# Counting SyncE's issue time per load as measured in a build-time ordering

## The chip, the cores and the metric

The kernel runs on one core of one Trainium2 chip. The metric is the time of one execution on the device in microseconds (us). A trace shows one execution, taken by the hardware profiler; its span is some 2 us shorter than the time of that execution. In it PE is TensorE's matmuls, PEld TensorE's weight loads, DVE VectorE, ACT ScalarE, POOL GpSimd, and SP SyncE. SyncE only issues transfers. A "landing" is the moment at which a transfer's data has arrived and its semaphore is raised.

## The reference

Threshold attention over 8 batches of 8 heads, 576 positions and 64 dimensions, then a gated feed-forward block with a folded RMS norm on the 4608 tokens:

```python
scores = scale * np.matmul(q, k.transpose(0, 1, 3, 2))
thresh = np.max(scores, axis=-1, keepdims=True) - tau           # tau = 0.02
scores = np.where(scores >= thresh, scores, -1e9)
attn = softmax(scores)
x = np.matmul(attn, v)                     # then heads to the last axis: [4608, 512]
xn = x / rms(x) * rms_g
g, val = xn @ w_gate, xn @ w_val           # 512 -> 1536
return (g * sigmoid(g) * val) @ w_out      # 1536 -> 512
```

## The kernel before

The scores are computed in fp32, the rest of the matmuls in fp16. Every piece of work is an `Op` with an engine, a cost in ns, a priority and its dependencies. A list scheduler puts them all into one order at build time. It walks through a model of the engines and always takes the op that can start first. Only that order goes to the chip. Each engine then runs its instructions in that order and waits on semaphores for what the model misjudged.

```python
COST = dict(
    s_main=932.0, s_virt=900.0, tr_qk=530.0, tr4=230.0, ...
    sp=350.0, sp_tr=1300.0, sp_qk=1310.0, sp_tl=630.0,
)
DMA_NS = dict(qk=1250.0, tl=700.0, v=880.0, vt=350.0, wt=1700.0, ..., w=820.0, wo=2500.0)
...
def order_ops(ops, ring_sizes):
    ...
                if o.bulk:                                   # loads: at most 3.5 us of transfers outstanding
                    t = max(t, dma_free - BACKLOG)
                k = (t + (BIAS if other else 0.0), o.prio, i)
    ...
        eng_free[e] = t + cost
        if o.dma:
            dma_free = max(dma_free, t + 300.0) + o.dma      # one pipe for all transfers
            o.end = max(dma_free, t + o.cost) + (LAT_TR if o.cost == COST["sp_tr"] else LAT_LD if o.bulk else 2000.0)
```

q and k are loaded in natural layout, k first and q after it. TensorE transposes them in groups of 16 (8 for k, then 8 for q) with priority -500, that is, as soon as the model takes both loads to have landed. v and the feed-forward weights are loaded on the same SyncE queue.

```python
def emit_qk(b, p, prio):                       # pair p of heads, batch b
    for j, src in ((1, k), (0, q)):
        def load(o, j=j, src=src):
            for h in range(2):
                nc.sync.dma_start(out=nat[:, j, :, h], in_=src[b, 2 * p + h, 0:MAIN].rearrange(...))
        los.append(gated(add("SP", COST["sp_qk"], prio - 3, before, load, dma=DMA_NS["qk"], bulk=True), prio - 3))
    def tr(o):                                 # 16 small fp32 transposes into two PSUM banks
        for j in (1, 0):
            for c in range(4):
                for r, rs in enumerate(HALF):
                    nc.tensor.transpose(ring[o.slot[r]][:, at:at + 64], nat[rs, j, c].rearrange(...), id32[rs, rs])
    t = gated(add("PE", COST["tr_qk"], -500.0, los + [o_id] + ..., tr, ring="R", nring=2, mode=1), prio)
...
def emit_v(b, prio):
    lo = gated(add("SP", COST["sp"], pr, ..., load, dma=DMA_NS['v'], bulk=True), pr)
...
# 24 weight loads
lo = gated(add("SP", COST["sp"], pr, w_use[slot][-1:], load, dma=DMA_NS['w'], bulk=True), pr)
...
seq = order_ops(ops, {"R": 4})
with tc.manual_schedule():
    for o in seq:
        o.fn(o)
```

A *step* below is one of 144 softmax steps. It begins with a *burst* of eight score matmuls (`s_ps<-qkt`). Transposes of the attention weights (`ring<-id,wsb`), attention-times-value matmuls (`ring<-va,wt`) and feed-forward groups (`ring<-xnT,wg`) fill the space between bursts.

## Time and profile before

| what | value |
|---|---|
| time, median of 3 runs (range) | 572.69 us (572.63 to 573.38) |
| span of the profiled run (its time) | 569.2 us (571.37 us) |
| busy PE / ACT / DVE | 98% / 81% / 75% |
| first and last score matmul of a main burst | 6.4 and 505.9 us |

The profile is shown in the prediction, line by line. In a time line a row is the start in us, the length in us, engine, source line, operation, output and inputs, and how many instructions. The square bracket is the idle time of the engine just before, with the releaser that the profile infers.

### The profile page before, as it was taken

The page shows a single profiled execution, that of the slowest core. Times are in us where ns is not written, and L with a number is a line of the kernel's source. Part 1 is how long each engine was busy: PE and PEld are TensorE (multiplying, and loading weights), DVE is VectorE, ACT ScalarE, POOL GpSimd, SP SyncE. Part 2 cuts the span into 40 slices and gives each one's busy share as a digit, 9 for nine tenths or more (in the row PEclk, how much of TensorE's full clock was granted, in tenths as well). Part 3 has the DMA queues.
Part 4 walks back from the last instruction along what each step waited for, and adds up shares of the span by engine and source line. Part 5 has one row for each costly group of instructions (what it writes and reads, how often), then busy time and mean ns, then how long its engine had stood idle before and what let it go on. Part 6 is the DMA issues. An engine that isn't in the chain of part 4 may idle for free.

```text
span 569.2 us, 13800 instructions
## 1 busy us (share of the span) xinstructions
PE 558.1 (98%) x5000; PEld 335.6 (59%) x5000; DVE 427.7 (75%) x1093; ACT 458.9 (81%) x739; POOL 322.2 (57%) x462
## 2 busy tenths in 40 slices
PE   8989999999999999999999999999999999999996
PEld 4666776767667555555555455555555555554674
DVE  4898986969868588858984888668974887486354
ACT  4998889998879888989888899789897898783331
POOL 2368956875657456665666557666674665451000
PEclk9999999999999999999999999999999999999999
DMA  7999999778896678889996688879977645641211
GB/s 180 233 271 261 227 172 218 142 121 186 184 200 121 130 149 158 186 181 162 175 180 157 134 168 174 186 176 176 179 157 185 95 94 106 141 107 30 75 39 37
DMA packets 271172, 89.00 MB, mean 156 GB/s; under 512 B 253696, under 2 KB 263424, under 8 KB 271104
## 3 DMA queue, kind: packets, MB, share of 16 engines
q1 hardware_dynamic: 268304, 86.02, 72.6%
q0 software_dynamic: 1600, 1.57, 1.9%
q8 instruction: 39, 0.64, 0.5%
q10 hardware_dynamic: 1200, 0.52, 0.3%
q14 instruction: 29, 0.24, 0.2%
HBM read 37.75 MB, written 9.44 MB: 83 GB/s over the span
## 4 chain that ended last, share of the span: by engine, by line
PE 88%; DVE 4%; DMA 3%; ACT 1%; SPq 1%; issue 1%; POOL 1%; ACTq 0%; DVEq 0%
PE s_ps L568 27%; PE ring L794 15%; PE ring L799 15%; PE ring L855 15%; PE ring L699 6%; PE ring L304 2%; DMA qkn<-in_q_dram 2%; PE ring L695 2%; DVE ssb L591 2%; PE s_ps L794 1%; PE s_ps L833 1%; PE s_ps L855 1%; PE ring L661 1%; PE s_ps L799 1%; ACT ssb L609 1%
## 5 line engine op out<-in xcount | busy, mean ns | idle before, releaser
L591 DVE CUSTOM_DVE_ANT_0 ssb<-s_ps,zrow 128x576 f32<-128x576 f32 x288 | 207.1, 753 | 56.6 <-PE s_ps L568 45.4
L609 ACT ACTIVATE ssb<-ssb,nth 128x576 f32<-128x576 f32 x224 | 165.4, 765 | 25.3 <-POOL nth L598 24.9
L568 PE MATMUL s_ps<-qkt 64*128 64x288 f32 x1024 | 170.9, 430 | 1.4 <-DVE mx L591 1.2
L568 PEld LDWEIGHTS s_ps<-qkt 64*128 64x128 f32 x1024 | 95.9, 186 | 53.0 <-DVE mx L591 16.8
L642 POOL TENSOR_SCALAR wsb<-ssb,nth 128x576 f16<-128x576 f32 x64 | 110.5, 1726 | 11.2 <-ACT esb L628 3.5
L799 PE MATMUL ring<-xnT,wv 128*128 128x512 f16 (+1 forms) x544 | 111.8, 328 | 0.1
L794 PE MATMUL ring<-xnT,wg 128*128 128x256 f16 (+1 forms) x540 | 111.0, 328 | 0.2 <-DVE hf L816 0.2
L598 POOL TENSOR_SCALAR nth<-mx 128x2 f32<-128x2 f32 x144 | 31.6, 220 | 126.9 <-DVE mx L591 116.7
L811 DVE SCALAR_TENSOR_TENSOR sl<-th,ring 128x512 f32<-128x512 f32 (+1 forms) x135 | 74.5, 552 | 28.8 <-ACT th L808 28.3
L616 ACT ACTIVATE wsb<-ssb 128x1152 f16<-128x1152 f32 x80 | 92.9, 1162 | 2.0
L808 ACT ACTIVATE th<-ring 128x512 f32<-128x512 f32 (+1 forms) x135 | 65.3, 485 | 31.0 <-PE ring L794 27.3
L855 PE MATMUL ring<-wo,hf 128*128 128x512 f16 x384 | 89.3, 380 | 0.0
L647 POOL TENSOR_TENSOR wsb<-wsb,esb 128x576 f16<-128x576 f16 x64 | 81.8, 1278 | 10.7 <-ACT esb L628 6.5
L816 DVE TENSOR_TENSOR hf<-ring,sl 128x512 f16<-128x512 f32 (+1 forms) x136 | 76.1, 560 | 12.0 <-PE ring L799 2.3
L794 PEld LDWEIGHTS <-wg 128*128 128x128 f16 x576 | 51.4, 98 | 45.0 <-issue 16.2
L799 PEld LDWEIGHTS <-wv 128*128 128x128 f16 x576 | 52.8, 98 | 39.7 <-issue 8.1
L855 PEld LDWEIGHTS <-hf 128*128 128x128 f16 x408 | 37.6, 98 | 47.1 <-issue 6.2
L699 PE MATMUL ring<-va,wt 128*128 128x65 f16 (+1 forms) x1264 | 52.8, 193 | 0.0
L628 ACT ACTIVATE esb<-ssb,nth 128x576 f16<-128x576 f32 x64 | 49.1, 767 | 3.3 <-POOL nth L598 3.2
L699 PEld LDWEIGHTS <-wt 128*128 128x128 f16 (+1 forms) x1280 | 48.7, 100 | 3.8
L613 ACT ACTIVATE wsb<-ssb 128x576 f16<-128x576 f32 x64 | 43.6, 681 | 1.5
L695 PE MATMUL ring<-va,wt 128*128 128x130 f16 (+1 forms) x158 | 35.1, 227 | 0.0
(68 smaller groups left out, 451.4 us busy)
## 6 DMA issues: line engine op xcount, KB each, us to landing
vst<-in_v_dram SPq DMA_DIRECT2D x32, 256.0 KB, 3.4
qkn<-in_k_dram SPq DMA_DIRECT2D x62, 128.0 KB, 3.2
out_dram<-osb SPq DMA_DIRECT2D x31, 256.0 KB, 2.6
qkn<-in_q_dram SPq DMA_DIRECT2D x56, 128.0 KB, 3.2
stage<-in_moe_w_gate_dram SPq DMA_DIRECT2D x12, 256.0 KB, 4.1
stage<-in_moe_w_val_dram SPq DMA_DIRECT2D x12, 256.0 KB, 4.4
wt<-wsb SPq DMA_TRANSPOSE x128, 3.1
wo<-in_moe_w_out_dram POOLq DMA_DIRECT2D x4, 384.0 KB, 6.1
```

The source lines that it names most:

```text
L568: nc.tensor.matmul(s_ps[h][rows, ROW_AT + n * part:ROW_AT + n * part + n], lhs(hs), kT[i][p][h][hs, n * part:n * part + n], start=True, st ...
L591: nc.vector.tensor_tensor_reduce(out=ssb[a][:, h], in0=s_ps[h][:, ROW_AT:ROW_AT + S], in1=zrow, scale=-1.0 / 8.0, scalar=3.0e38, op0=ALU.a ...
L609: nc.scalar.activation(out=ssb[a][:, h], in_=ssb[a][:, h], func=PRELU, scale=-1.0, bias=nth[m][:, h:h + 1], **PRELU_KW)
L616: nc.scalar.activation(out=wsb[s % NW], in_=ssb[a], func=AF.Exp)
L642: nc.gpsimd.tensor_scalar(out=wsb[s % NW][:, h], in0=ssb[a][:, h], scalar1=nth[m][:, h:h + 1], scalar2=None, op0=ALU.is_le)
L647: nc.gpsimd.tensor_tensor(out=wsb[s % NW][:, h], in0=wsb[s % NW][:, h], in1=esb[es], op=ALU.mult)
L699: nc.tensor.matmul(ring[o.slot[0]][rs, at:at + D + 1], w[:, 5 * h + j, rs], va[vi][:, p, 2 * j + h], start=False, stop=(h == 1 and j == 3))
L794: nc.tensor.matmul(ring[o.slot[0]][:, 0:n], wg[d][:, fs], xnT[slot][:, d, 0:n], start=(d == 0), stop=(d == 3))
L799: nc.tensor.matmul(ring[o.slot[0]][:, 0:n], wv[d][:, fs], xnT[slot][:, d, 0:n], start=(d == 0), stop=(d == 3))
L811: nc.vector.scalar_tensor_tensor(out=sl[i][:, 0:n], in0=th[i][:, 0:n], scalar=1.0, in1=ring[g.slot[0]][:, 0:n], op0=ALU.add, op1=ALU.mult)
L816: nc.vector.tensor_tensor(out=hf[hi][:, 0:n], in0=ring[vv.slot[0]][:, 0:n], in1=sl[i][:, 0:n], op=ALU.mult)
L855: nc.tensor.matmul(ring[(first or o).slot[0]], hf[hs[fc][0]][:, 128 * j:128 * (j + 1)], wo[:, fc], start=(fc == 0), stop=(fc == NFC - 1))
```

## The change

SyncE's issue time was counted as 350 ns for every plain load and store. The trace has more: 412 to 434 ns at the median for a weight load and 582 for a v load. The change counts 480, and 650 for v. The intent is that the model then expects loads later, so that transposes of q and k stand behind later score bursts and don't make TensorE wait for data. No instruction is added or removed.

```diff
-    sp=350.0, sp_tr=1300.0, sp_qk=1310.0, sp_tl=630.0,
+    sp=480.0, sp_v=650.0, sp_tr=1300.0, sp_qk=1310.0, sp_tl=630.0,
...
-            lo = gated(add("SP", COST["sp"], pr, v_cast[...] ..., load,
+            lo = gated(add("SP", COST["sp_v"], pr, v_cast[...] ..., load,
                            dma=DMA_NS['v'], bulk=True), pr)
```

More of the change, by code (lines that the diff above doesn't have):

```diff
@@ L500, in load @@
                 nc.sync.dma_start(out=nat, in_=main[:, 2 * p:2 * p + 2])
-            lo = gated(add("SP", COST["sp"], pr, v_cast[n - len(vst):n - len(vst) + 1] if n >= len(vst) else [], load,
+            lo = gated(add("SP", COST["sp_v"], pr, v_cast[n - len(vst):n - len(vst) + 1] if n >= len(vst) else [], load,
                            dma=DMA_NS['v'], bulk=True), pr)
```

## The prediction

> **What bounds the kernel now.** I read the page first: busy shares, then the 40 slices.
>
> ```profile
> span 569.2 us, 13800 instructions
> PE 558.1 (98%) x5000; PEld 335.6 (59%) x5000; DVE 427.7 (75%) x1093; ACT 458.9 (81%) x739; POOL 322.2 (57%) x462
> ...
> PE   8989999999999999999999999999999999999996
> ...
> PEclk9999999999999999999999999999999999999999
> ```
>
> TensorE has work in 558.1 of 569.2 us at full clock. All its idle time together is 569.2 - 558.1 = 11.1 us, 1.9% of the span. A change that only moves instructions about can hardly take more than that. The view of busy time by stretches tells where the idle time lies:
>
> ```profile
> 0.00:45.00 45.00, 39.89 (x378) 27.14 (x378) 34.09 (x98) 35.61 (x54) 19.63 (x45) 1.00 0.92 230
> 45.00:80.00 35.00, 34.69 (x336) 25.03 (x334) 30.70 (x88) 31.88 (x53) 27.18 (x43) 1.00 1.16 228
> 80.00:508.00 428.00, 426.67 (x3907) 247.93 (x3905) 329.97 (x837) 369.98 (x589) 272.13 (x370) 1.00 0.79 158
> 508.00:569.20 61.20, 56.84 (x389) 35.51 (x387) 32.98 (x73) 21.42 (x45) 3.28 (x6) 0.98 0.17 49
> ```
>
> (The columns are length, then busy PE, weight load, DVE, ACT, POOL, granted clock, DMA share, GB/s.) The first 45 us hold 45.00 - 39.89 = 5.1 us of idle time, and the last 61 us hold 61.20 - 56.84 = 4.4. The 463 us between hold only 11.1 - 5.1 - 4.4 = 1.6 us. The last stretch is the feed-forward drain, without loads of q, k or v, so the change has no handle on it. Next, what the transposes of q and k wait for, from the view of the tile that they read:
>
> ```profile
> L304 PE MATMUL ring<-id,qkn x448: 216/222/273, 22.5 to 423.0; 64*128 64x64 f32 x150
> ...
> its engine sat idle before it (us, times) until:
>   DMA qkn<-in_q_dram: 5.2, 5
> ```
>
> The 5.2 us count both the matmul row and the weight-load row for the same stalls (5 entries). The waits split them: 2.6 us over 3 waits on the matmul row, 2.5 over 2 on the weight-load row. So it is three places, and the time line of PE shows them:
>
> ```profile
> 22.50 0.41 PE L304 MATMUL ring<-id,qkn 64*128 64x64 f32 x8
> 23.20 0.46 PE L304 MATMUL ring<-id,qkn 64*128 64x64 f32 x8 [0.30 <-DMA qkn<-in_q_dram]
> 24.44 0.43 PE L440 MATMUL ring<-id,ktl 64*128 64x64 f32 x4 [0.77 <-DVE qkt L317]
> ...
> 36.94 0.46 PE L304 MATMUL ring<-id,qkn 64*128 64x64 f32 x8 [1.28 <-DMA qkn<-in_q_dram]
> ...
> 153.63 0.46 PE L304 MATMUL ring<-id,qkn 64*128 64x64 f32 x8 [1.05 <-DMA qkn<-in_q_dram]
> ```
>
> Each time, the k half of a transpose group has run, and the q half waits for its load. That is the prize: 0.30 + 1.28 + 1.05 = 2.6 us, plus 0.77 us for a tail transpose that waits for the DVE copy of the late group. 3.4 us in all, 0.6%.
>
> **Why the transposes stand too early.** The kernel orders its instructions at build time with a model of each engine; the change alters two constants of it. The trace has what they stand for:
>
> ```profile
> L500 SPq DMA_DIRECT2D vst<-in_v_dram x32: 415/582/2029, 7.4 to 430.2; - x32
> ...
> L918 SPq DMA_DIRECT2D stage<-in_moe_w_gate_dram x12: 327/412/628, 21.0 to 55.1; - x12
> L918 SPq DMA_DIRECT2D stage<-in_moe_w_val_dram x12: 328/434/1275, 21.7 to 61.7; - x12
> ```
>
> The model counts 350 ns for each. The medians are 582 ns (v) and 412 to 434 ns (weights), and consecutive weight loads start at 21.69, 22.17, 22.64 us, 470 to 480 ns apart. So 480 for loads and 650 for v are nearer to the chip than 350, and the model at present thinks SyncE ahead of where it is.
>
> **What the Trainium skill says.** Three places.
> - "Perfetto Trace Analysis", section "Per-instruction lifecycle: what the profiler-reported window actually captures": for a DMA issued by SP the reported window is the descriptor generation and not the data movement. The trace agrees: a q load's issues take 628 ns at the median, while the landing comes 3.2 us after issue.
> - "DMA: Bandwidth & Descriptors", section "Rules for kernel authors": issue the DMA early, compute, and wait on its semaphore late. A transpose placed later is the last third of that rule. The trace agrees in that only three of 28 such groups stall.
> - "TensorE: Matmul & The Clock Gate", section "Part 2: What happens when you issue a matmul": matmuls stay in program order and only weight loads are pulled ahead. The three stalls show it: a q half that waits stops the score bursts after it, although these read other buffers.
>
> **The change, part by part.** No instruction is added or removed, and every duration on the chip stays: 448 + 28 + 28 + 32 small fp32 transposes, 1280 score matmuls, 24 weight loads, 32 v loads, 39 stores on SyncE. Only the order on each queue can differ.
> - Model time added: 24 weight loads x 130 ns = 3.1 us, 32 v loads x 300 ns = 9.6 us, some 31 stores x 130 ns = 4.0 us; 16.7 us over the kernel.
> - Start-up: 16 weight loads and 3 v loads are issued between 16.6 and 45 us, and 4 v loads before. If SyncE is the model's bottleneck there, the later transposes shift by up to 16 x 0.13 + 7 x 0.30 = 4.2 us. But the model also charges the DMA pipe 820 ns per weight load and 880 per v load, more than the new issue times, and holds bulk loads when 3.5 us of transfers are outstanding; where that holds, the shift is nil. I take half, 2 us.
> - A softmax step in this part is some 3 us (the score bursts start at 18.04, 21.43, 25.41, 27.79 and 31.13 us), so a shift of 2 us puts most transpose groups of batch 1 behind one further score burst of 1.2 us. The 0.30 and the 1.28 us then vanish behind work that PE has anyway, and probably the 0.77. Expected: 2.35 us x 0.7 = 1.6 us.
> - Steady state: per pair of transposed inputs the added time is one v load or two, 0.3 to 0.6 us. The stall at 153.63 is 1.05 us long. A choice at a burst boundary may flip or not; I take half of it, 0.5 us.
> - A cost in turn: later transposes mean later copies to SBUF (685 ns on DVE, 567 on ACT). Batch 1 is first needed at step 16, near 57 us, and its transposes run between 22.5 and 45 us, so 3 us more lateness hits nothing. The three staging buffers free later by the same shift, which can delay a later load by a step; SyncE has waits of tens of us in front of its transposes, so I count nothing.
> - Reshuffling: the order also decides how score bursts, feed-forward groups and evacuations mesh for 500 us. PE there is full, and any new order can open or close some tenths of a us in many places. I take the mean as zero and the size as about 3 us either way, since the present tuned order leaves only 1.6 us in 463.
> Sum: -1.6 - 0.5 = -2.1 us, so 572.7 - 2.1 = 570.6 us.
>
> **The rivals.**
> 1. *Stall removed, all paid back.* In the first 80 us PE is not alone: DVE has 34.1 of 45 us and then 30.7 of 35, ACT 35.6 and 31.9. PE's weight loads wait 6.4 us for DVE's row reductions there. If the softmax chain paces that part, PE arrives earlier only to wait for DVE. For it: those waits. Against it: the lost PE time is never made up later, because PE is full from 57 us on, so work done earlier shortens the end. Time: 572 to 573.
> 2. *The order hardly changes*, because the model's DMA pipe and not SyncE sets the load times. For it: 820 and 880 ns against 480 and 650. Against it: q and k loads cost 1310 ns on SyncE against 1250 on the pipe, so SyncE counts there, and the change is described by moved transposes. Time: 572.5.
> 3. *A new wait*: a load or store that is chosen differently on SyncE stands in front of an attention-weight transpose (1306 ns each, 128 of them), and attention-times-value matmuls then wait. For it: one in-order queue, which carries everything. Against it: nearly all waits on that queue are for ACT and POOL, so it has slack. Time: 574 to 580.
> 4. *All stalls vanish*, the model now fits the chip and the drain starts earlier: 572.7 - 3.4 = 569.3, with lucky meshing 566.
>
> **Range and chances.** The middle is 570.6. The floor is near 558.1 + 4.4 + some 1.5 us before the first input lands, about 564 in the span, or 567 with the 3.5 us between span and time (572.69 - 569.2); I set the low end a little below, at 566.5. The high end, rival 3 in a mild form, is 575.0. Faster by over 2% means under 561.2, which would need PE idle time of zero: 0.01. Slower by over 2% means above 584.1, an ordering accident of 12 us: 0.03. Within 2%: 0.96.
>
> **What would show it.** Right: the waits of the q/k transposes for the q load fall from 2.6 us to under 1 on the matmul row; the score burst that stood behind the group at 36.9 now precedes it; PE idle in the first 45 us falls from 5.1 to 3 or 4; counts and mean durations of all groups are the same; PE busy stays within 2 us of 558. Wrong: waits of the same size at other transposes or on the v and weight casts, a gap on PE before the attention-times-value matmuls, or a longer drain after the last score burst (now 505.9 to 569.2 us). The prediction falls if the idle time between 80 and 508 us grows above 4 us, or if the end moves by more than the sum of the stalls.

## The result and the profile after

| | median us | range | runs |
|---|---|---|---|
| before | 573.24 | 572.63 to 575.65 | 6 |
| after | 573.86 | 573.39 to 575.79 | 6 |

The ratio of after to before is 1.0011, with a 95% interval of 0.9989 to 1.0033: the same, and if anything 0.6 us slower, where 2.1 us of gain were forecast. Ratios here are the mean time of one kernel's fast runs over the mean of the other's fast runs of the same rounds, so they are not quite the ratios of the quoted medians. Where I turn a ratio into us, I multiply its difference from 1 by the median of before.

The page of after and its busy time by stretches:

```profile
span 571.9 us, 13796 instructions
...
PE 557.3 (97%) x5000; PEld 333.3 (58%) x5000; DVE 427.6 (75%) x1093; ACT 460.2 (80%) x739; POOL 323.5 (57%) x462
```

```profile
0.00:45.00 45.00, 39.38 (x360) 26.06 (x361) 33.34 (x97) 34.13 (x53) 17.98 (x42) 1.00 0.86 216
45.00:80.00 35.00, 33.06 (x340) 24.28 (x337) 29.85 (x84) 30.57 (x50) 27.83 (x45) 1.00 1.06 219
80.00:508.00 428.00, 425.03 (x3890) 245.78 (x3887) 328.20 (x832) 368.72 (x587) 270.10 (x366) 1.00 0.79 159
508.00:571.90 63.90, 59.85 (x422) 37.20 (x420) 36.19 (x84) 26.74 (x53) 7.59 (x12) 1.00 0.20 56
```

The work is the same (PE 557.3 us against 558.1, the same number of instructions on the five engines). The columns are those of the prediction. The idle time of PE per stretch is its length minus PE's busy time (the number after the comma):

| stretch | before | after |
|---|---|---|
| 0 to 45 | 5.11 | 5.62 |
| 45 to 80 | 0.31 | 1.94 |
| 80 to 508 | 1.33 | 2.97 |
| 508 to end | 4.36 | 4.05 |
| sum | 11.11 | 14.58 |

So idle time did not shrink in the first 45 us, and new idle time came in the 463 us after that. The time line of PE in after, with its longer waits at transposes and feed-forward groups:

```profile
24.89 0.24 PE L440 MATMUL ring<-id,ktl 64*128 64x64 f32 x1 [1.43 <-DVE wt L670]
...
38.00 0.46 PE L304 MATMUL ring<-id,qkn 64*128 64x64 f32 x8 [1.26 <-DVE wt L670]
38.85 0.46 PE L304 MATMUL ring<-id,qkn 64*128 64x64 f32 x8 [0.39 <-DMA qkn<-in_q_dram]
...
53.50 0.60 PE L794 MATMUL ring<-xnT,wg 128*128 128x256 f16 x4 [1.30 <-POOL nth L598]
...
157.71 0.47 PE L304 MATMUL ring<-id,qkn 64*128 64x64 f32 x8 [0.99 <-DMA qkn<-in_q_dram]
```

One more wait, between 80 and 508 us, stands in front of an attention-times-value group:

```profile
180.75 0.22 PE L695 MATMUL ring<-va,wt 128*128 128x130 f16 x1 [1.01 <-ACT qTv L474]
```

It comes back in every other trace with the order of after (0.78 us in after_again, 1.17 in after_fix, 0.90 in after_pad_pe, all near 179 us). The order of before has none there (its second trace has one of 0.73 us at 165.83).

The releasers in the brackets have to be checked. For each of the five waits of the first list I looked for a landing of the tile that the instruction reads. There is one each time, some 0.13 us before the start: the tail of k of the batch (`ktl`) at 24.76, k of pair 2 at 37.86, q of it at 38.72, `xnT`, a transposing transfer issued at 46.90, at 53.37, and the q load at 157.58. So where the profile names DVE or POOL, it was a transfer. The same check on before changes one reading of the prediction: its 0.77 us at 24.44 "for a tail transpose that waits for the DVE copy" was a wait for the load of `ktl` too, which landed at 24.30. That load in before, read from the view of the tile:

```profile
L428 SPq DMA_DIRECT2D ktl<-in_k_dram x1: 631/631/631, 20.3 to 20.3; - x1
...
DMA to landing us min/median/max: 4.0/4.0/4.0
```

Waits of q and k transposes that a landing ended come to 0.30 + 0.77 + 1.28 + 1.05 = 3.4 us in before. In after they are 1.43 + 1.26 + 0.39 + 0.28 (at 47.23) + 0.99 = 4.35 us, and a feed-forward group that the new order starts earlier waits 1.30 us for `xnT`. The view of the tile of q and k in after says it in short, without the `ktl` stall; its idle times count matmul and weight-load rows together, as in the prediction:

```profile
L304 PE MATMUL ring<-id,qkn x448: 216/222/273, 26.0 to 431.3; 64*128 64x64 f32 x150
...
its engine sat idle before it (us, times) until:
...
  DVE wt L670: 2.7, 2
  DMA qkn<-in_q_dram: 2.2, 4
```

The group that had stalled at 22.50 to 23.20 now runs behind the next burst (at 25.98, behind the burst that starts at 24.91), and does not wait. That part worked as intended. But the tail transposes now stand alone before that burst and wait. The stall of pair 2 did not go away in this trace, although the model had been told to expect loads later. One reason is in the trace: its loads were issued later as well, and landed later still. First before, then after (the two issues of k of pair 2, for two heads):

```profile
L294 SPq DMA_DIRECT2D qkn<-in_k_dram x2: 630/686/742, 29.6 to 30.4; - x2
...
DMA to landing us min/median/max: 4.5/4.6/4.8
```

```profile
L294 SPq DMA_DIRECT2D qkn<-in_k_dram x2: 570/600/629, 31.6 to 32.3; - x2
...
DMA to landing us min/median/max: 5.6/5.7/5.8
```

The issue moved by 2.00 us (29.65 to 31.65) and the landing by 2.95 (34.91 to 37.86). The queue already ran late at the first pair of this batch (k issued at 18.07, in before at 16.60), and one more weight load (31.06) now stands in front of pair 2. The group itself did not pass a burst: it stands in front of the burst of step 10 in both kernels (37.94 and 39.12 us), only the weight transposes at 37.33 now come before it (36.06).

The first and the last of the score matmuls in before, then in after:

```profile
L568 PE MATMUL s_ps<-qkt x1024: 402/403/507, 6.4 to 505.9; 64*128 64x288 f32 x171
```

```profile
L568 PE MATMUL s_ps<-qkt x1024: 402/403/507, 6.8 to 514.1; 64*128 64x288 f32 x171
```

The last score matmul moved by 8.2 us, the end by 2.7. Feed-forward work stands between earlier bursts and the drain is shorter. The position of a burst in the middle therefore says little about the end.

### The profile page after: what moved, and what is told of

It reads as the page before. It is cut to its first block, busy times and chain, and to the rows that moved or that the text cites. A ratio compares the mean times of both kernels' runs of the same rounds, so it can differ in the third digit from the quotient of the medians.

```text
span 571.9 us, 13796 instructions
## 1 busy us (share of the span) xinstructions
PE 557.3 (97%) x5000; PEld 333.3 (58%) x5000; DVE 427.6 (75%) x1093; ACT 460.2 (80%) x739; POOL 323.5 (57%) x462
## 4 chain that ended last, share of the span: by engine, by line
PE 81%; DMA 6%; ACT 4%; POOL 3%; DVE 2%; issue 2%; SPq 1%; DVEq 0%; POOLq 0%; ACTq 0%
PE s_ps L568 24%; PE ring L855 15%; PE ring L794 14%; PE ring L799 14%; PE ring L699 5%; DMA stage<-in_moe_w_gate_dram 2%; PE ring L695 2%; DMA wt<-wsb 2%; PE ring L304 2%; ACT ssb L609 1%; DVE ssb L591 1%; PE s_ps L799 1%; PE s_ps L833 1%; PE ring L366 1%; PE s_ps L855 1%
## 5 line engine op out<-in xcount | busy, mean ns | idle before, releaser
L568 PE MATMUL s_ps<-qkt 64*128 64x288 f32 x1024 | 168.6, 429 | 1.5 <-DVE mx L591 1.3
L794 PE MATMUL ring<-xnT,wg 128*128 128x256 f16 (+1 forms) x564 | 114.3, 325 | 1.3 <-POOL nth L598 1.3
L799 PE MATMUL ring<-xnT,wv 128*128 128x512 f16 (+1 forms) x528 | 110.4, 331 | 0.3 <-DVE xsb L717 0.2
L811 DVE SCALAR_TENSOR_TENSOR sl<-th,ring 128x256 f32<-128x256 f32 (+1 forms) x141 | 77.2, 547 | 33.9 <-ACT th L808 33.4
L808 ACT ACTIVATE th<-ring 128x256 f32<-128x256 f32 (+1 forms) x141 | 67.8, 481 | 31.2 <-PE ring L794 25.1
L855 PE MATMUL ring<-wo,hf 128*128 128x512 f16 x384 | 89.8, 380 | 0.0
L799 PEld LDWEIGHTS <-wv 128*128 128x128 f16 x576 | 52.1, 98 | 43.1 <-issue 12.5
```

The costliest lines, as they stand in the source:

```text
L568: nc.tensor.matmul(s_ps[h][rows, ROW_AT + n * part:ROW_AT + n * part + n], lhs(hs), kT[i][p][h][hs, n * part:n * part + n], start=True, st ...
L794: nc.tensor.matmul(ring[o.slot[0]][:, 0:n], wg[d][:, fs], xnT[slot][:, d, 0:n], start=(d == 0), stop=(d == 3))
L799: nc.tensor.matmul(ring[o.slot[0]][:, 0:n], wv[d][:, fs], xnT[slot][:, d, 0:n], start=(d == 0), stop=(d == 3))
L811: nc.vector.scalar_tensor_tensor(out=sl[i][:, 0:n], in0=th[i][:, 0:n], scalar=1.0, in1=ring[g.slot[0]][:, 0:n], op0=ALU.add, op1=ALU.mult)
L855: nc.tensor.matmul(ring[(first or o).slot[0]], hf[hs[fc][0]][:, 128 * j:128 * (j + 1)], wo[:, fc], start=(fc == 0), stop=(fc == NFC - 1))
```

## The experiments

Three theories stood against each other.

1. *Placement*: TensorE bounds the whole kernel, so a stall that goes is time gained (the prediction's).
2. *Slack at the start*: in the first 50 us TensorE waits for landings, wherever the transposes stand. Taking a stall away only shows the next wait, and TensorE work there costs nothing.
3. *Downstream*: the stalls were gained, and the new order lost them again later.

Five lots of kernels ran, each with its own runs of before.

### The same programs again

No edit: before and after, as they are, under new names.

> The kernel before, unchanged: what a second profile of the same program differs by. Both theories: time within 0.3% of the kernel before; the three stalls of TensorE at the transposes of q and k (1.28 us near 37 us, 1.05 near 154, 0.3 to 0.8 near 23) come again within 0.3 us if they belong to the order; if they move about by a microsecond between executions, single profiles can't carry an argument of 1 us.

> The changed kernel, unchanged, beside the rest on one chip. Time 573.9 us or so, 0 to 0.3% over the kernel before. If the late weight load (issued near 29.2, landed near 36.0) belongs to the order, it lands 6 to 7 us after issue again and TensorE stands some 1.3 us near 38 us; if it was an accident of that execution, it lands after 4 us and the profile shows a start-up some 1 to 2 us shorter.

| | median us | before | ratio (95%) | profiled span |
|---|---|---|---|---|
| before_again | 572.55 | 572.94 | 0.9992 (0.9974 to 1.0010) | 572.3 |
| after_again | 573.33 | 572.94 | 1.0004 (0.9987 to 1.0021) | 570.8 |

The time of after is again that of before, to 0.2%. The profiles are the surprise: the same program had a span of 569.2 in its first profile and 572.3 in its second (before), and 571.9 and 570.8 (after). The 2.7 us between the first pair of traces is no more than one program differs from itself, and the first trace of before was of a fast execution (571.37 us, below all six of its timed runs in the result). In the second trace of before, the k half of pair 2 starts after 0.86 us of idle time and the q half waits 2.00 us, and during that wait TensorE loses clock (the granted clock is 0.53 from 37 to 38 us). Its time line, and the stretches with the granted clock in the third column from the right:

```profile
35.79 0.46 PE L304 MATMUL ring<-id,qkn 64*128 64x64 f32 x8 [0.86 <-DMA qkn<-in_k_dram]
38.25 0.69 PE L304 MATMUL ring<-id,qkn 64*128 64x64 f32 x8 [2.00 <-DMA qkn<-in_q_dram]
```

```profile
38.00:42.00 4.00, 3.75 (x25) 2.59 (x25) 1.45 (x3) 3.07 (x4) 1.35 (x3) 0.50 0.95 252
```

The q load had landed at 38.12 where it was 36.80 in the first trace. The burst of step 11 starts at 44.15 us instead of 40.32. Some 3 us of it are still there at the end. The 1.05 us near 154 us are absent in this trace.

The second trace of after answers the question that was put to it. The weight load issued at 28.89 us lands after 4.78 us where it took 6.84 in the first trace, so that landing was an accident of one execution. The group of pair 2 does not wait at all. Yet the burst of step 11 starts at 41.31 us, only 0.17 earlier: the tail transposes wait longer instead, and TensorE then has half the clock until 29 us.

```profile
25.23 0.24 PE L440 MATMUL ring<-id,ktl 64*128 64x64 f32 x1 [2.05 <-DMA ktl<-in_k_dram]
```

```profile
25.62:29.02 3.40, 3.40 (x35) 2.97 (x33) 1.37 (x3) 1.55 (x4) 2.78 (x4) 0.50 1.11 306
```

In the second pair of traces the waits of q and k transposes come to 0.36 + 0.86 + 2.00 = 3.2 us in before and 2.05 + 0.58 = 2.6 us in after. With 3.4 and 4.35 us in the first pair, they neither vanish nor clearly grow. So single profiles can name the waits of a run, but they cannot carry a difference of 2 us. For that I use timed rounds only.

### Which constant moves the order

```diff
# v_only                          # w_only
-    sp=350.0, ...                -    sp=350.0, ...
+    sp=350.0, sp_v=650.0, ...    +    sp=480.0, sp_v=350.0, ...
```

Both have the second line of the change as well.

> Only the v loads are counted longer (650 ns); all else 350. The order that comes out puts the transposes of batch 1 exactly where the full change puts them up to 50 us, and differs from before in 116 of 652 TensorE groups. Theory D (the moved transposes merely wait for another load): the wait at the k-tail transposes near 24 us is 1.4 to 2 us, as in the changed kernel, the sum of TensorE's stalls in the first 45 us is not below before, and the time is within 1 us of before. Theory A (transposes placed later gain their stall): 570 to 571.5.

> Only weight loads and stores are counted longer (480 ns), v loads stay at 350. The order that comes out is that of before on TensorE in all 652 groups, and differs on SyncE in 15 of 346. Both theories: within 1 us of before (0.2%). More than 2 us either way would mean that the order of a few loads on SyncE alone moves the time.

| | median us | before | ratio (95%) |
|---|---|---|---|
| v_only | 573.85 | 572.60 | 1.0021 (0.9997 to 1.0044) |
| w_only | 571.48 | 572.60 | 0.9985 (0.9960 to 1.0010) |

Compared instruction group by group, w_only has the very TensorE order of before (0 of 652 groups differ) and differs on SyncE in 15 of 346. v_only differs from before in 116 TensorE groups, and has the TensorE order of after up to 50 us. So by itself the v constant moves the transposes of the first 50 us, and the tail transposes of v_only wait 1.95 us, as expected. The weights' constant, which the prediction charged with 16 x 0.13 us of the shift, moves no transpose by itself. The two do not simply add up: rebuilt from the kernels, v_only and after differ in 404 of the 652 TensorE groups, from the 51st on. Both intervals contain 1, so neither kernel differs measurably from before.

### One queue's order of one kernel, the rest of the other

```diff
-    seq = order_ops(ops, {"R": 4})
+    before, after = both_orders(ops)     # the two orders, from the old and the new issue times
+    seq = merged(after, before)          # rest_after: SyncE as in before, all other engines as in after
+    seq = merged(before, after)          # sp_after: SyncE as in after, all other engines as in before
```

Where the two do not fit together, a needed transfer is pulled forward (5 in sp_after), so these are not pure halves.

> SyncE's queue in the order of before, every other engine in the order of after. Theory A (the moved loads cost what the moved transposes gain): loads land as early as before while the transposes stand later, so waits for q and k loads fall under 1 us and the time is 1 to 3 us below before, 570 to 572. Theory B (the place of the transposes is worth nothing, because the start is paced by the softmax chain): within 0.7 us of before. Theory C (the order of the other engines itself is worse): 1 us or more above before.

> SyncE's queue in the order of after (five loads pulled forward where the two orders don't fit together), every other engine in the order of before. Theory A: loads land later and transposes stand as early as before, so waits at the transposes grow to 5 us or more and the time is 2 to 4 us above before. Theory B: no more than 1 us above before. Theory C: within 0.7 us of before.

| | median us | before | ratio (95%) |
|---|---|---|---|
| rest_after | 593.96 | 572.94 | 1.0367 (1.0346 to 1.0387) |
| sp_after | 597.43 | 572.94 | 1.0433 (1.0409 to 1.0457) |

None of the theories had this loss of 21 and 25 us. It doesn't come from the start: the burst of step 56 starts at 199.32 and 203.74 us (before: 197.02), the last one at 533.02 and 531.84 (before: 505.07). A late stretch shows part of it, first rest_after, then sp_after:

```profile
440.00:508.00 68.00, 63.26 (x511) 32.09 (x510) 43.37 (x107) 50.34 (x78) 34.27 (x46) 0.92 0.45 98
```

```profile
440.00:508.00 68.00, 60.39 (x488) 30.14 (x484) 42.35 (x104) 47.75 (x74) 32.66 (x46) 0.95 0.44 100
```

TensorE is idle for 4.7 and 7.6 of 68 us there, in which before and after have 68.00 busy of 68, and it has lost clock besides. SyncE is one in-order queue that carries loads, attention-weight transposes and stores. My reading, which no run tests, is that a queue order fits only the order of the other engines that it was made with; in sp_after TensorE waits 8.4 us for attention-weight transposes after 80 us. The prediction's third rival named that danger (574 to 580 us); after itself does not have it, since all queues are ordered together. As a test of what the changed SyncE order does by itself the two runs fail, because the misfit covers it.

### The stalls taken away by hand

In the finished order, the stalling transposes are moved behind the next burst, with what reads them:

```diff
+    bursts = {id(o) for o in s_of.values()}
+    for op in (MARK["kt", 1], MARK["qk", 1, 2], MARK["qk", 3, 2]):   # after_fix: and the first feed-forward group
+        seq = behind(seq, op, bursts)
```

SyncE's order stays as it is. In before_fix this is what the change was meant to do, without its side effects.

> The kernel before with three transpose groups (k tail of batch 1, pair 2 of batch 1, pair 2 of batch 3) moved behind the next burst of score matmuls, SyncE untouched: the prediction's effect by itself. If a stall at a transpose is worth its length: the three waits (0.4 to 0.8, 1.3 to 2.9 and 0 to 1.05 us in two profiles of before) vanish, and the time falls by 2 to 4 us, to 569.5 to 571.5. Rival (the start is paced by DVE and ACT, so the stall only changes its owner): waits vanish from the transposes, but the time stays within 1 us of before.

> The changed kernel with its k-tail transposes, the first feed-forward group, and the same two transpose groups moved behind the next burst: it takes away the stalls that the change brought (1.4 to 2.0 us near 25, 0.75 to 1.3 near 53, up to 1.0 near 156). If the change's gain was eaten by these: 2 to 4 us below the changed kernel, and 1.5 us or more below before. Rival (stalls at the start are worth nothing): within 1 us of the changed kernel.

| | median us | before | ratio (95%) |
|---|---|---|---|
| before_fix | 572.04 | 572.60 | 0.9992 (0.9970 to 1.0015) |
| after_fix | 572.92 | 572.60 | 1.0021 (0.9989 to 1.0052) |

Three stalls with 0.77 + 1.28 + 1.05 = 3.1 us were removed from before, and the gain is 0.5 us, between 1.7 of gain and 0.9 of loss. The time line of PE in before_fix, then that of ACT:

```profile
36.48 0.68 PE L678 MATMUL ring<-id,wsb 128*128 128x128 f16 x9 [1.60 <-ACT wsb L633]
...
40.26 1.19 PE L585 MATMUL s_ps<-qkt 64*128 64x288 f32 x4 [0.24 <-DVE mx L608]
```

```profile
35.26 1.16 ACT L633 ACTIVATE wsb<-ssb 128x1152 f16<-128x1152 f32 x1
```

TensorE now reaches the weight transposes of the step sooner, and waits 1.60 us for the exponential that ends at 35.26 + 1.16 = 36.42. The burst of step 11 starts at 40.26 us, in before at 40.32. Here the wait has changed its name and nothing else. In that trace a wait of 0.88 us at 24.26 stands in place of the 0.77, and one of 0.66 us at 45.71 is new. The third stall, at 153.63, lies outside the start. In this trace nothing takes its place: idle time from 80 to 508 us is 0.36 us, against 1.33 in before. Whether that one us is part of a real gain, the interval cannot say.

### Slack, measured by added work

TensorE gets 32 needless matmuls, 128x128 by 128x512 in fp16, written to a PSUM bank that is overwritten next. Once in steps 4 to 11, once in steps 57 to 72:

```diff
# pad_pe_start, after_pad_pe          (in the weight transposes)
+                if 4 <= s < 12:
+                    for _ in range(4):
+                        nc.tensor.matmul(ring[o.slot[0]], zrow[:, 0:128], zrow[:, 0:512], start=True, stop=True)
# pad_pe_late                         (in the attention-times-value group, every second step)
+            if 57 <= s < 73:
+                for _ in range(4):
+                    nc.tensor.matmul(...)               # the same
```

> The kernel before with four more 128x128 by 128x512 matmuls of zeros in front of the weight transposes of steps 4 to 11, order unchanged, result unchanged. Estimate: 8 steps of 4 matmuls at 0.22 us, 6.9 us of work added to TensorE's queue in the start-up. If a stall of TensorE there is worth its length (the prediction's step), the time rises by 6 to 7 us, to 578.5 to 580 (1.0% to 1.2%). If ACT and DVE pace the score steps there and TensorE has slack, the work lies in gaps: 0 to 3 us (up to 0.5%).

> The control: the same 8 times four matmuls, in front of the attention-times-value groups of steps 57 to 71 (200 to 255 us), where TensorE shows no idle time. Both theories: 6 to 7 us more (1.0% to 1.2%). Less than 4 us would mean that busy time there hides slack too.

> The changed kernel with the 6.9 us of zero matmuls of pad_pe_start. If TensorE has the same slack in the start-up of the changed order: within 1.5 us of the changed kernel (573.3 to 573.9 in two rounds of runs). If the change used it up: 4 us or more above.

| | median us | before | ratio (95%) |
|---|---|---|---|
| pad_pe_start | 571.87 | 573.26 | 1.0007 (0.9966 to 1.0047) |
| pad_pe_late | 580.53 | 573.26 | 1.0130 (1.0103 to 1.0157) |
| after_pad_pe | 573.86 | 572.95 | 1.0027 (0.9998 to 1.0057) |

The added matmuls are the same in both places. First pad_pe_start, then pad_pe_late:

```profile
L661 PE MATMUL ring<-zrow x32: 377/379/390, 26.4 to 52.1; 128*128 128x512 f16 x32
```

```profile
L691 PE MATMUL ring<-zrow x32: 379/379/390, 215.6 to 273.7; 128*128 128x512 f16 x32
```

The 379 ns are a matmul from end to end, and they overlap. As an estimate of their cost: the 384 output-projection matmuls of the same shape have 89.8 us of busy time in after, 0.234 us each, so 32 cost 7.5 us; at the 0.216 us of the cost table, 6.9. Placed late they cost 0.0130 x 573.26 = 7.4 us. Placed at the start they cost 0.0007 x 573.26 = 0.4 us, with an interval from 1.9 us of gain to 2.7 of loss. **Some 7 us of TensorE work in steps 4 to 11 are free** within that interval. The added work stands between 26.4 and 52.1 us; the stall of 1.28 us lies there, that of 0.77 just before, and that of 1.05 at 153.63 does not. after_pad_pe has 573.86 us, as after had, so the changed order leaves the same room. One rival can be set aside from the record: the added work could be free because it keeps the clock up. But span x (1 - granted clock), listed for every execution, averages 0.95 us in the six runs of pad_pe_start and 0.99 in the eleven of before. The busy view hid the slack. pad_pe_start's stretches:

```profile
0.00:45.00 45.00, 41.58 (x380) 27.13 (x381) 33.10 (x96) 34.65 (x54) 19.81 (x46) 1.00 0.92 229
45.00:80.00 35.00, 35.00 (x351) 25.87 (x351) 30.77 (x88) 31.88 (x51) 26.87 (x42) 1.00 1.09 223
```

In before the second stretch had 34.69 us busy of 35, so it looked full. With the added matmuls the first 80 us hold 41.58 + 35.00 = 76.58 us of busy time, and before had 39.89 + 34.69 = 74.58: 7 us of work raised it by 2.0. A burst of eight score matmuls takes 1.24 us where nothing holds it, and 1.60 and 1.77 us in others (before, at 31.13 and 40.32), while its weight loads wait for VectorE (0.24 us at 40.85). The matmuls of such a burst start further apart, but as each lasts 0.4 us or more they still overlap, and the whole burst counts as busy.

The same question for the other engines and for the transfers, all in steps 4 to 11:

```diff
# pad_act_start: eight copies on ScalarE (0.62 us each in the trace, 4.9 us)
+                        nc.scalar.copy(out=th[0], in_=zrow[:, 0:512])
# act_less_start: the exponential of half the width (0.5 us less each, eight times, 4.0 us); result wrong on purpose
-                    nc.scalar.activation(out=wsb[s % NW], in_=ssb[a], func=AF.Exp)
+                        nc.scalar.activation(out=wsb[s % NW][:, 0], in_=ssb[a][:, 0], func=AF.Exp)
# pad_dve_start: eight copies on VectorE (0.58 us each, 4.6 us)
+                    nc.vector.tensor_copy(out=th[0], in_=zrow[:, 0:512])
# pad_pool_start: eight on GpSimd (0.62 us each, 5.0 us)
+                nc.gpsimd.tensor_scalar(out=th[1], in0=zrow[:, 0:512], scalar1=1.0, scalar2=1.0, op0=ALU.mult, op1=ALU.mult)
# pad_dma_start: eight loads of 256 KB that nothing reads, issued by ScalarE
+                        nc.scalar.dma_start(out=junk, in_=moe_w_gate[128 * (s % 4):128 * (s % 4) + 128, 0:512])
```

> The kernel before with one more ACT copy of 128x512 (an estimate of 0.5 us) between the masking and the exponential of steps 4 to 11, 8 in all, 4 us of ACT work in the start-up. If ACT paces that part: 2.5 to 4 us more (0.4% to 0.7%), more than the 6.9 us of TensorE work cost in the run beside it. If TensorE paces it: under 1.5 us.

> Wrong result on purpose: in steps 4 to 11 the exponential handles one head of two, which takes 0.48 us (1.16 to 0.68) off ACT in each, 3.8 us in all; order unchanged. If ACT paces the start-up: 2 to 4 us less (0.35% to 0.7%). If the loads or TensorE pace it: within 1 us of before.

> One more DVE copy of 128x512 between the two row reductions of steps 4 to 11: 8 times an estimated 0.4 to 0.6 us, 3 to 5 us. If DVE sets the pace: 3 us or more (0.5%). If landings do: under 1.5 us.

> One more POOL operation of 128x512 (0.63 us by the v casts) in front of the threshold of steps 4 to 11: 5 us of POOL, on the way from the row minimum to the masking. If POOL, whose queue also holds the casts that wait for weight loads, sets the pace: 3 us or more. If landings do: under 1.5 us, or up to 2.5 as it also lengthens the softmax chain.

> The kernel before with eight more loads of 256 KB (2.1 MB) in steps 4 to 11, issued from ACT's queue into tiles that are not yet in use; order and result unchanged. At the 261 GB/s that the DMA engines moved between 20 and 45 us that is an estimate of 8 us of transfers. If landings set the length of the start-up: 4 to 8 us more (0.7% to 1.4%). If not: under 1.5 us.

| | median us | before | ratio (95%) |
|---|---|---|---|
| pad_act_start | 572.36 | 573.26 | 0.9995 (0.9968 to 1.0022) |
| act_less_start | 574.18 | 573.26 | 1.0011 (0.9982 to 1.0041) |
| pad_dve_start | 572.62 | 572.95 | 0.9993 (0.9967 to 1.0019) |
| pad_pool_start | 572.18 | 572.95 | 0.9996 (0.9970 to 1.0022) |
| pad_dma_start | 575.93 | 572.95 | 1.0077 (1.0043 to 1.0111) |

Some 5 us of work on ScalarE, VectorE or GpSimd are free, too (by the intervals they cost at most 1.3 us), and 4.0 us less on ScalarE gain nothing measurable. (act_less_start's relative error is 0.27; every other kernel's result was correct.) Only the transfers cost: 2.1 MB more take 0.0077 x 572.95 = 4.4 us (2.5 to 6.4). In its trace TensorE also lost clock for a while:

```profile
0.00:45.00 45.00, 38.69 (x352) 26.10 (x353) 31.64 (x92) 32.89 (x51) 18.08 (x42) 0.96 0.98 243
...
40.00:42.00 2.00, 2.00 (x13) 0.97 (x10) 0.84 (x3) 0.97 (x2) 1.55 (x3) 0.50 1.07 372
```

So the runs point to the transfers as what paces the start; no single compute engine does, each tried alone. It is not shown: the same loads were not added late in the kernel as a control. Later landings and the clock after a stall are mixed in the 4.4 us, but the record bounds the second. Span x (1 - granted clock) averages 3.9 us in the six runs of pad_dma_start and 1.15 in the eleven of before, so as an estimate at most 2.8 of the 4.4 us are clock.

### Fewer loads in the crowded part

If transfers pace the start, spreading the weight loads might help. From before, with the priorities of the 24 weight loads changed:

```diff
# wstep_05: spaced further              # wfrom_4: beginning later
-W_STEP = 0.4                           -W_FROM = 2.0
+W_STEP = 0.5                           +W_FROM = 4.0
```

> The kernel before with the 24 weight loads spaced 0.5 steps apart, not 0.4 (the last one some 2.4 steps later). If landings set the start-up and the q and k loads gain from the thinner stream: 1 to 2.5 us less (0.2% to 0.4%). If only the sum of the bytes up to the first feed-forward work counts: within 1 us of before.

> The kernel before with the weight loads allowed from step 4 on, not 2. Same two theories: 1 to 2.5 us less if the q and k loads of batch 1 gain, within 1 us if the sum of the bytes counts, and 1 to 3 us more if the feed-forward work then starts late.

| | median us | before | ratio (95%) |
|---|---|---|---|
| wstep_05 | 573.41 | 572.56 | 1.0019 (0.9998 to 1.0040) |
| wfrom_4 | 571.60 | 572.56 | 0.9989 (0.9968 to 1.0011) |

Neither differs measurably from before, so spacing the weight loads at this size is not the remedy, and which loads set the pace stays open. The edits also move TensorE groups (119 and 234 of 652, rebuilt from the kernels), so they do not test the spacing alone. No version was found that beats both kernels.

### Where the bursts stand

Starts of score bursts in us, from one trace of each kernel:

| step | before | before_again | before_fix | pad_pe_start | pad_dma_start | after | after_again |
|---|---|---|---|---|---|---|---|
| 11 | 40.32 | 44.15 | 40.26 | 42.09 | 43.42 | 41.48 | 41.31 |
| 24 | 80.73 | 83.60 | 82.85 | 82.00 | 85.30 | 86.75 | 86.17 |
| 56 | 197.02 | 200.09 | 198.77 | 197.22 | 200.67 | 199.98 | 198.57 |
| 143 | 505.07 | 508.15 | 506.82 | 505.28 | 508.72 | 513.26 | 512.14 |
| end | 569.25 | 572.32 | 570.99 | 569.15 | 573.28 | 571.92 | 570.78 |

The kernels with the order of before keep their distance from step 24 to the end to about half a us, apart from pad_pe_start, whose lag of 1.3 us is down to 0.2 by step 56. In these kernels the spread at the end is made before 80 us. There landings differ from run to run (q of pair 2: 36.80 and 38.12 in the same program). Why they differ I have not found out.

## Why the prediction was right or wrong

**Right.** The time stayed within 2% and in the range. Counts and durations stayed. PE's busy time moved by 0.8 us, within the 2 forecast. The drain did not lengthen. The idle time from 80 to 508 us grew to 2.97 us, below the 4 that would have meant a broken order. Of the rivals the first (stall removed, all paid back, 572 to 573 us) came nearest in outcome. Its reason, the softmax chain, is not what the runs show: added work on any one engine of that chain cost nothing measurable. That the time lies in the range is owed to the width of the range, as the gain behind its middle did not come. Two of the prediction's own signs of being wrong did come: a wait at other transposes (1.43 us at `ktl`) and a gap before attention-times-value matmuls (1.01 us at 180.75).

**Wrong: the gain of 2.1 us.** Two terms made it, and neither came.

- *"The 0.30 and the 1.28 us then vanish behind work that PE has anyway, and probably the 0.77 ... 2.35 us x 0.7 = 1.6 us."* Two things failed in it.
  - The stalls did not vanish. In the first trace the 0.30 went, the 0.77 became 1.43 at the same tail transposes, and the 1.28 became 1.26 + 0.39 at the same group, which passed no burst and whose loads were issued 2.00 us later. In the second trace the 1.28 went too, but the tail transposes waited 2.05. I treated load times on the chip as fixed while only transposes moved. But the constant sits in the model of the queue that issues the loads, and so moves them as well.
  - Even where stalls do vanish, no gain can be measured. before_fix removed three stalls, two of them (0.77 + 1.28 = 2.05 us) in this part, and gained 0.5 us (-0.9 to 1.7).
- The failed premise is the argument against the first rival: *"the lost PE time is never made up later, because PE is full from 57 us on, so work done earlier shortens the end."* It takes for granted that TensorE time saved at the start brings the end forward. The runs show that it doesn't: pad_pe_start has some 7 us of free room there, while pad_pe_late pays 7.4 us for the same work. Each compute engine alone had room, and only transfers cost, so the runs point to the loads as what sets the length of the start; that last step is argued, not shown.
- *The 0.5 us of the steady state* for half the stall at 153.63: in after it is at 157.71 with 0.99 us instead of 1.05, at the same group. It was absent in the second trace of before and 0.58 us in that of after.

**Misread.** The 0.77 us was a wait for a load, not for the DVE copy that the profile named. Of the shift of up to 4.2 us in model time, the 16 x 0.13 us of the weight loads moved no transpose by themselves (w_only). The 3.5 us "between span and time" under the low end compared a trace with other executions: the profiled execution took 571.37 us, 2.2 more than its span. *"PE idle in the first 45 us falls from 5.1 to 3 or 4"*: it was 5.62.

**Whether something was lost downstream.** The trace of after has a wait of 1.30 us at 53.50 for `xnT`, 0.75 us in its second trace. But after_fix moved that group and was no faster than before (572.92 against 572.60), so this wait did not eat a gain. after_fix left the wait near 180 us in place (1.17 us), some 35 us before the part where pad_pe_late paid for TensorE work, and no run takes it away by itself. Between 80 and 508 us TensorE is idle for 1.8 to 3.0 us in the four traces with the order of after (after_fix among them), and for 0.3 to 2.4 us (1.1 at the mean) in the ten with that of before and no work added there (w_only and before_fix among them). So a loss of about one us downstream is not excluded. It would be of the size of the 0.6 us by which after is slower, and too small to stand for the whole gain of 2.1 us.

**Open.** What sets each landing in the crowded first 80 us; how much of pad_dma_start's loss, up to 2.8 us, is clock; what the wait near 180 us costs; why spans of one program differ by 3 us; and whether after is truly 0.6 us slower or the same, since its interval holds both.

## What to carry to other kernels

Before you count a stall as time to be had, add as much work to that engine in that part: if the time stays, the engine has slack there and the stall is a symptom, however full the busy view looks. Add the same work where you expect none to be free, as a control. A constant in an ordering model that describes a queue moves the queue's own transfers as well as those that wait for them, so read the issue and the landing of the load before you judge the new place of the wait. Know how much the profile of one unchanged program differs from another of the same (3 us here) before you explain 2 us by two traces.

## What the Trainium skill lacked or had wrong

- The Trainium skill, "TensorE: Matmul & The Clock Gate", section "Why this matters for your kernels", advises against PE-idle gaps over some 3 us, since one idle window brings half the clock. Here shorter ones were enough: after the one gap of 2.05 us that ended at 25.23 us in the second trace of after, the granted clock was 0.50 from 25.62 to 29.02 us. In the second trace of before it was 0.50 from 38 to 42 us, with gaps of 0.86 and 2.00 us and 0.46 us of transposes between them. A gap of 1.95 us in v_only, and gaps of 1.26 and 0.39 us in after, left it at 1.00.
- The Trainium skill, "DMA: Bandwidth & Descriptors", section "Anatomy of one DMA — SWDGE (gpsimd) path", gives a fit of 2.0 us plus bytes over 436e3 for one transfer issued by GpSimd. An estimate from it for 256 KB is 2.6 us. The loads of `w_gate` of that size, issued by SyncE beside other loads, took 4.1 us at the median in before and 4.5 in after, and one took 6.84 us. The section has no figure for loads issued by SyncE, and the page none for the time from issue to landing of a load beside others.
- The Trainium skill, "Perfetto Trace Analysis", section "Identifying the Most-Contended Engine", says that matmul busy time is not a good measure of how close TensorE is to its limit, and the runs agree that it hides room. It doesn't offer the test that settled it here: some 7 us of added matmuls raised the busy time of the first 80 us by 2.0 us and the kernel's time by nothing measurable.
- No page mentions a check of a releaser that the profile infers: compare the end of the wait with the landings of the tile that is read. Waits put down to VectorE and GpSimd (1.43, 1.26 and 1.30 us in after) each ended some 0.13 us after such a landing.
